# Output projection in fifteen products per unit for seven per pair of hidden tiles, with sums that read one operand from PSUM and a new written order

## The chip, the cores and the metric

One core of a Trainium2 chip runs the whole program. The metric is device time in microseconds (us) of one execution, the median of three runs. Engines are called TensorE (PE in the profile, its weight loads PEld), VectorE (DVE), ScalarE (ACT), GpSimd (POOL) and SyncE (SP, which here only issues DMAs).

## The reference, cut to what matters

```python
# x: (8, 4096, 192), weight: (8, 7); 32768 tokens in all
w = softmax(weight, axis=-1)                 # 8 heads of 24 channels, 7 taps
y[b, s, h] = sum_k w[h, k] * x_pad[b, s + k, h]   # causal depthwise convolution
xn = y / sqrt(mean(y * y) + 1e-6) * rms_g    # over the 192 channels
g, val = xn @ w_gate, xn @ w_val             # 192 -> 1536 each
out = (g * sigmoid(g) * val) @ w_out         # 1536 -> 192
```

All in float32 on the chip; the weights of the second block come as float64 and are converted at the start.

## The kernel before, in words

The tokens are worked in 32 pairs of two token tiles of 512 (T). Pair 0 is done plainly (L1060, L1101) behind the setup; pairs 1 to 31 go through one loop that follows a written order, `ORDER`. A pair's hidden width of 1536 is 12 tiles of 128, taken as four units of three tiles.

**Input stage.** A unit's gate and val sums (3 blocks of 64 channels by 3 hidden tiles by 2 token tiles, 18 block products) are made by 15 products of sums, `Unit.product` (L798). Gate uses the lower 64 rows of the array and val the upper 64, so that the two run side by side. The moving operands are the blocks of xn in `xb` (six: three channel blocks by two token tiles) and ten sums of them in `xc`, written `X0` to `X10` in the order (`x_sum`, L705 to L709): on GpSimd (`G`), on VectorE (`V`), or by a copying DMA from SP and an accumulating DMA that GpSimd issues (`Q`). The products accumulate in PSUM banks; half 0 is gate, half 1 val. Actions of `Unit.do` move between banks and tiles: `S` a snapshot of a bank (L747 on ScalarE, L751 on VectorE), `F` a copy from one bank into a new one, `D`, `C`, `N` and `R` sums on VectorE that take a bank and a tile (L814, L824, L818, L830), `G` a SiLU on ScalarE (L843) and `M` the multiplication of SiLU and val into the hidden tile `ht` (L850).

**Output stage.** Here 2x2 blocks (token tile by neighbouring hidden tiles, hidden tiles by column halves) are multiplied by 7 products for 8 in place of the plain way. Their left sides are hidden tiles and sums of them, made by `Pair.sum` (L968 to L970; `S1` to `S4` in the order), their right sides blocks of `w_out` and sums of them, made once (`out_sums`, L864). 42 steps, each of six matmuls of 384, 256 or 128 columns on four quarters of 32 columns of the array (`Pair.tile`, L938), accumulate in three banks X, Y, Z. `c1`, `s7`, `c2` copy among them, `C22` and `C21` join (L991), `T11` to `T22` turn 32x32 blocks into row order (L953), and `st0`, `st1` store.

**Work ahead.** In the same order, VectorE makes the convolution of the pair after the next (`cv`, L476, seven taps by three parts that accumulate in three PSUM banks), then `sq` (ScalarE), `red`, `pow` (GpSimd), `bc`, `mul` (GpSimd, L530) make the norm, `place` stores it to DRAM, and `fetA`, `fetB` load the next pair's blocks into `xb` (L696).

**Order.** A word of `ORDER` is an engine letter, an action, a half and a unit (`GM1.0.2`: GpSimd, multiplication of hidden tile 1 of unit 2). `p2` issues the next two of the pair's products. A minus sign at the end means that the action belongs to the pair before. Each engine runs its own instructions in the order in which they are written, and waits only where data or buffers ask for it; so the order of words sets each engine's queue, not the time. `D` words go to SP's queue. PSUM has eight banks in two groups of four (`free`), handed out as the order is written.

Of the kernel before, what the change touches and what calls it, by code (L numbers as in the profile page):

```python
# [19 lines left out]
def kernel(  # L20
# [99 lines left out]

# [1197 lines left out]
```

## Time and profile before

| quantity | value |
|---|---|
| median of 3 runs | 2594.6 us (2593.61 to 2594.77) |
| span of the profiled execution | 2591.7 us |
| the same execution's idle TensorE | 11.4 us (busy 2580.3) |
| VectorE, ScalarE, GpSimd busy | 2273.3, 1554.2, 2078.6 us |
| granted clock of TensorE | 1.000 |
| first pair of the loop starts | 125.77 us |
| products of TensorE by line, share of the chain | L798 62%, L938 32%, L1060 2%, L1101 1% |

The span runs from the first to the last instruction; the median lies 2.9 us above it, and this is taken as fixed. The chain that ended last follows the work back from the last instruction, at each step to what released it. A group's mean time is that of one instruction from its start to its end; successive instructions of an engine overlap, so the time from start to start is shorter.

### The profile page before, as it was taken

The numbers are of one execution on the slowest core, as the hardware profiler recorded it, in microseconds if no ns is written. First come the engines' busy times: TensorE is split into PE (matmuls) and PEld (weight loads), VectorE is DVE, ScalarE is ACT, GpSimd is POOL, SyncE is SP. The second block draws the span as 40 slices with busy tenths as digits, with TensorE's granted clock in tenths as the row PEclk, the third lists the DMA queues.
The fourth block names the chain that finished last, engine by engine and source line by source line (L and its number), as shares of the span: only waits on it lengthen the run. The fifth ranks groups of instructions, "written<-read, shape, count | busy, mean of one in ns | idle before, by whom it ended". The sixth has DMA issues, their size and how long they took to land.

```text
span 2591.7 us, 61274 instructions
## 1 busy us (share of the span) xinstructions
PE 2580.3 (100%) x23872; PEld 1777.6 (69%) x23872; DVE 2273.3 (88%) x3681; ACT 1554.2 (60%) x2825; POOL 2078.6 (80%) x1791
## 2 busy tenths in 40 slices
PE   9999999999999999999999999999999999999999
PEld 6876666767667666676666676666766666766666
DVE  8899989888889988889889889898988898898975
ACT  6566555675555765556755557655567555676554
POOL 4887788887778877788877888778888788887777
PEclk9999999999999999999999999999999999999999
DMA  6243554334553335443345433354433455334431
GB/s 145 57 83 59 100 100 87 75 65 90 100 100 77 72 68 104 99 83 77 65 91 100 98 76 69 74 104 96 86 76 66 92 100 94 72 72 80 91 76 22
DMA packets 555887, 216.54 MB, mean 84 GB/s; under 512 B 488782, under 2 KB 491342, under 8 KB 555598
## 3 DMA queue, kind: packets, MB, share of 16 engines
q1 hardware_dynamic: 525644, 164.00, 30.7%
q0 software_dynamic: 26208, 47.72, 10.9%
q8 instruction: 187, 3.06, 0.5%
q10 hardware_dynamic: 3746, 0.92, 0.2%
q14 instruction: 102, 0.84, 0.1%
HBM read 83.84 MB, written 49.55 MB: 51 GB/s over the span
## 4 chain that ended last, share of the span: by engine, by line
PE 98%; DMA 1%; POOL 0%; DVE 0%; issue 0%; SPq 0%; DVEq 0%; POOLq 0%
PE ps L798 62%; PE ps L938 32%; PE ps L1060 2%; PE ps L1101 1%; DMA xb<-xd 0%; POOL tls L970 0%; DMA xc<-xb 0%; DVE xb L647 0%; POOL more L970 0%; SPq L696 0%; DVE wf L338 0%; POOL xc L706 0%; DVE xc L333 0%; DVE o_sb L953 0%; DVE xc L298 0%
## 5 line engine op out<-in xcount | busy, mean ns | idle before, releaser
L798 PE MATMUL ps<-xc,wf 64*128 64x512 f32 x4960 | 1214.6, 591 | 0.0
L798 PEld LDWEIGHTS ps<-xc,wf 64*128 64x128 f32 x4960 | 681.6, 186 | 375.3 <-issue 161.8
L798 PE MATMUL ps<-xb,wf 64*128 64x512 f32 x2480 | 680.3, 591 | 0.0
L747 ACT ACTIVATE tile<-ps 128x512 f32<-128x512 f32 x678 | 391.0, 593 | 388.3 <-PE ps L798 282.7
L747 ACT ACTIVATE tls<-ps 128x512 f32<-128x512 f32 (+1 forms) x562 | 323.5, 588 | 438.9 <-PE ps L798 209.9
L850 POOL TENSOR_TENSOR ht<-ht,tile 128x512 f32<-128x512 f32 x329 | 419.2, 1278 | 125.4 <-ACT tile L843 48.9
L798 PEld LDWEIGHTS ps<-xb,wf 64*128 64x128 f32 x2480 | 354.2, 187 | 182.7 <-issue 91.9
L970 POOL TENSOR_TENSOR early<-ht 128x512 f32<-128x512 f32 x279 | 374.7, 1343 | 42.2 <-DMA ht<-ht 37.3
L850 POOL TENSOR_TENSOR ht<-ht,tls 128x512 f32<-128x512 f32 x260 | 331.2, 1279 | 76.9 <-ACT tls L843 33.2
L747 ACT ACTIVATE ps<-ps 128x512 f32<-128x512 f32 (+1 forms) x589 | 336.1, 581 | 87.6 <-PE ps L938 32.5
L476 DVE SCALAR_TENSOR_TENSOR ps<-xh,tp,ps 128x512 f32<-128x512 f32 x450 | 320.6, 750 | 3.9 <-ACT ps L468 1.7
L938 PE MATMUL ps<-ht,wo_sb 128*32 128x128 f32 (+2 forms) x5208 | 318.3, 380 | 0.0
L938 PEld LDWEIGHTS ps<-ht,wo_sb 128*32 128x32 f32 x5208 | 233.8, 110 | 81.7 <-issue 22.0
L938 PE MATMUL ps<-ht,x 128*32 128x128 f32 (+2 forms) x4464 | 250.7, 379 | 0.0
L830 DVE TENSOR_TENSOR tile<-ps,tile 128x512 f32<-128x512 f32 x349 | 237.8, 684 | 10.2 <-PE ps L798 5.4
L830 DVE TENSOR_TENSOR ht<-ps,tile 128x512 f32<-128x512 f32 x328 | 223.0, 682 | 6.4 <-ACT tile L747 6.4
L938 PEld LDWEIGHTS ps<-ht,x 128*32 128x32 f32 x4464 | 184.4, 110 | 61.2
L843 ACT ACTIVATE tile<-tile 128x512 f32<-128x512 f32 x349 | 214.5, 625 | 0.0
L830 DVE TENSOR_TENSOR ht<-ps,tls 128x512 f32<-128x512 f32 x292 | 199.4, 683 | 6.8 <-ACT tls L747 3.6
L830 DVE TENSOR_TENSOR tls<-ps,tls 128x512 f32<-128x512 f32 x271 | 185.2, 685 | 16.7 <-PE ps L798 13.6
L938 PE MATMUL ps<-early,x 128*32 128x256 f32 (+2 forms) x3348 | 196.0, 379 | 0.0
L938 PEld LDWEIGHTS ps<-early,x 128*32 128x32 f32 x3348 | 143.0, 110 | 44.6
(152 smaller groups left out, 3270.2 us busy)
## 6 DMA issues: line engine op xcount, KB each, us to landing
xb<-xd SPq DMA_DIRECT2D x120, 384.0 KB
xc<-xb SPq DMA_DIRECT2D x120, 256.0 KB
xd<-yn SPq DMA_DIRECT2D x244, 96.0 KB
xh<-in_x_dram SPq DMA_DIRECT2D x192, 105.0 KB
ht<-ht POOLq DMA_DIRECT2D x62, 256.0 KB, 3.3
xc<-xb POOLq DMA_DIRECT2D x60, 256.0 KB, 3.8
xc<-xc POOLq DMA_DIRECT2D x60, 256.0 KB, 4.0
out_dram<-o_sb SPq DMA_DIRECT2D x122, 96.0 KB
```

What stands on the lines that cost most here:

```text
L476: nc.vector.scalar_tensor_tensor(out=dst, in0=xk, scalar=w, in1=at, op0=ALU.mult, op1=ALU.add)
L747: nc.scalar.activation(out=dst, in_=src, func=AF.Copy, scale=float(s))
L798: nc.tensor.matmul(out=self.new(v, h, True) if first else self.old(v, h), lhsT=wf[self.u][HALF[h], WAT[i], :], rhs=x_op(XOP[i])[HALF[h]], ...
L830: nc.vector.tensor_tensor(out=self.hv(v) if h else t[:], in0=self.old(v, h), in1=t[:], op=plus(s))
L843: nc.scalar.activation(out=t[:], in_=src[:], func=AF.Silu)
L850: engine[eng].tensor_tensor(out=self.hv(v), in0=src, in1=t[:], op=ALU.mult)
L938: nc.tensor.matmul(out=self.bank(b)[i * Q : (i + 1) * Q, at : at + n], lhsT=left, rhs=cols, start=fresh, stop=True, skip_group_check=True, ...
L970: engine[eng].tensor_tensor(out=dst, in0=a, in1=b, op=op)
L1060: nc.tensor.matmul(out=bank(h, bks[h])[:], lhsT=wf[u][HALF[h], AT[h][k] * NF + f, :], rhs=xb[HALF[h], g, k, :], start=(k == 0), stop=(k == ...
L1101: nc.tensor.matmul(out=bank(h, bks[h])[:, w : w + D], lhsT=hts[f // NF][HALF[h], g, f % NF, j * P : (j + 1) * P], rhs=wo_sb[HALF[h], f, :] ...
```

## The change

The output stage goes over to 15 products per unit in place of 18: two token tiles by three hidden tiles by three column blocks of 64. A unit's six hidden tiles are called a to f. A product is four matmuls of 256 columns, one for each quarter; there are 60 in a pair, in the order of `OUTS`. They accumulate in K, R, N and four half banks C0, C1, C3, C4; `FORKS` copy among these, `SNAP` takes snapshots and `JOIN` adds them in. The left sides are made by `SUMS`: by GpSimd (`G`), by an accumulating DMA (`Q`), or by VectorE (`P`), which then takes its second operand from a PSUM bank into which ScalarE has copied it (`Ak...`). The same goes for two of the sums of x (`AkX3 PX3`, `AkX6 PX6`). Two val results of the last unit stay in their bank (`W`) until they are multiplied. Eleven sums of blocks of `w_out` are made in 18 steps, 12 ahead of pair 1 and 6 in it.

```diff
+    PLACE = {'a': 1, 'b': 0, 'c': 2, 'd': 4, 'e': 3, 'f': 5}
+    BANKS = {'K': 1, 'R': 1, 'N': 0, 'C01': 1, 'C34': 0}
+    OUTS = (
+        "11.1 11.0 6.0 6.2 4.1 6.1 6.3 11.2 4.2 1.0 1.2 11.3 4.0 4.3 14.3 9.0 8.0 8.1 8.2 9.1 9.3",
+        "9.2 14.2 14.1 5.0 8.3 10.0 5.3 10.3 5.1 5.2 3.1 13.2 13.1 3.3 7.0 7.3 13.0 10.1 7.1 10.2",
+        "7.2 13.3 1.3 14.0 12.0 3.0 2.1 12.1 12.3 12.2 1.1 3.2 0.3 2.2 2.0 0.1 0.2 2.3 0.0",
+    )
     ORDER = (
...
+        "VD6- VD0- GX5- GX10- p1 VT2- p1 GX9- VD2- VD3- VT4- p2 VT5- Asq- AS40.0.0 p2 AS40.1.0",
+        "VT3- p1 AF0.0.0 VT0- GX8- p1 VT1- VC.0.0 GX7- AF0.1.0 p3 VC.1.0 AS41.0.0 AS41.1.0 p1",
+        "AS00.0.0 p2 AS00.1.0 p2 GX4- p1 Vred- VD5.1.0 AS42.0.0 VD5.0.0 p1 AS42.1.0 VR1.0.0",
+        "VR0.0.0 Gpow- VR1.1.0 AS51.0.0 p1 AS51.1.0 p1 VR0.1.0 p1 Dload- Vbc- AF2.0.0 p1 AG0.0.0",
...
+        "AG4.0.0 GM2.1.0 VR5.1.0 VM4.1.0 AG3.0.0 p1 AF0.0.1 p1 GM3.1.0 p2 Gcb.0 p1 VS41.0.1 p1",
...
+        "VR5.1.3 AG5.0.3 p2 Qde.2 VR3.0.3 Qbe.2 AG4.0.3 VM4.1.3 p1 WR3.1.3 AG2.0.3 AG3.0.3 p1",
+        "Akp4.2 p2 GM1.1.3 VM3.1.3 p2 GM0.1.3 Akab.3 Akp9.0 Pp4.2 p2 AS6 GM5.1.3 Pab.3 p1 WR2.1.3",
+        "Gdf.3 Dplace- Akp4.0 Gde.3 Acv0_1 p2 DfetA DfetB p1 Pp4.0 p1 AF3 Gp4.3 Akp9.1 VM2.1.3",
+        "Qp9.2 p1 Pp9.0 Vcv1_1 Pp9.1 Gcb.3 p1 Gp9.3 p1 Vcv2_1 AF1 p1 Vcv3_1 Vcv4_1 p2 Akabe.1",
+        "Akbe.1 Vcv5_1 p1 Pabe.1 p2 Gabe.0 Gabe.2 p2 AF0 Acv0_2 Vcv6_1 p1 Qbe.3 p1 Pbe.1 p1",
+        "Vcv1_2 Akbce.0 p1 Qabe.3 p1 VS8 p3 AkX3 p1 Pbce.0 p1 AS5 Vcv2_2 p1 Gbce.3 Akbcf.1 Vcv3_2",
+        "PX3 p1 Gbce.2 p2 Gbce.1 Vcv4_2 p1 Vcv5_2 Vcv6_2 Acv0_0 Gbcf.0 QX0 Vcv1_0 Akabd.1 p2",
+        "Pbcf.1 Qabd.0 p2 AS7 Pabd.1 p2 Vcv2_0 Gbcf.2 p1 AS13 p2 Akbcf.3 Pbcf.3 VD13 AkX6 Akabd.2",
+        "p2 Qabd.3 p1 Vcv3_0 Vcv4_0 Pabd.2 Vcv5_0 p2 AF4 p1 Vcv6_0 p2 VD1 p1 GX1 p3 VD7 AS2 PX6",
+        "GX2",
     )
...
@@ x_sum
+        if eng == "A":
+            staged[i] = stage(x_op(b))
+            return
         e = nc.gpsimd if eng == "G" else nc.vector
+        e.tensor_tensor(out=xc[:, d, :], in0=x_op(a), in1=unstage(staged, i, x_op(b)), op=ALU.add)
+    def stage(src):
+        h = 0 if len(free[0]) >= len(free[1]) else 1
+        at = h, pick(h, False)
+        nc.scalar.copy(out=bank(*at)[:], in_=src)
+        return at
...
@@ Unit.do
+                stay = eng == "W"
+                dst = self.old(v, h) if stay else self.hv(v) if h else t[:]
+                nc.vector.tensor_tensor(out=dst, in0=self.old(v, h), in1=t[:], op=plus(s))
+                if not stay:
+                    self.leave(v, h)
...
+    VSUM = (
+        ("p11", "add", "01", "20"), ("p5", "sub", "11", "p11"), ("p8", "sub", "10", "p11"),
...
+    LEFT = {
+        11: ("X", "K"), 9: ("X", "K"), 5: ("CB", "K"), 7: ("CB", "K"), 12: ("CB", "K"),
+        4: ("S", "R"), 8: ("AB", "R"), 13: ("AB", "R"), 2: ("AB", "R"),
+        6: ("e", "N"), 1: ("b", "N"), 3: ("a", "C0"), 10: ("c", "C1"), 14: ("d", "C3"),
+        0: ("f", "C4"),
+    }
+    SUMS = {
+        "ab": ("AB", "a", "b"), "cb": ("CB", "c", "b"), "be": ("b", "b", "e"),
+        "df": ("X", "d", "f"), "de": ("X", "X", "e"), "p4": ("S", "AB", "X"),
+        "p9": ("X", "X", "CB"), "abe": ("AB", "AB", "e"), "abd": ("AB", "AB", "d"),
+        "bce": ("CB", "CB", "e"), "bcf": ("CB", "CB", "f"),
+    }
+    FORKS = {"F3": ("C3", "K", -1), "F1": ("C1", "R", 1), "F0": ("C0", "K", 1), "F4": ("C4", "K", -1)}
+    SNAP = {"S6": "N", "S8": "R", "S5": "K", "S13": "R", "S7": "K", "S2": "R"}
+    JOIN = {
+        "D0": ("C0", "S8", 1), "D1": ("C1", "S5", 1), "D13": ("N", "S13", -1),
+        "D7": ("N", "S7", -1), "D3": ("C3", "S2", -1), "D2": ("K", "S2", 1), "D6": ("K", "S6", -1),
+    }
...
@@ Pair.products
+            for w in " ".join(OUTS).split():
+                n, u = (int(i) for i in w.split("."))
+                src, b = LEFT[n]
...
+                cols, to = self.form(src, u), self.part(b)
+                for q in range(NQ):
+                    i, a = divmod(q, 2)
+                    nc.tensor.matmul(
+                        out=to[q * Q : (q + 1) * Q, :], lhsT=left[:, u, a],
+                        rhs=cols[:, i * HALFT : (i + 1) * HALFT], start=fresh, stop=True,
+                        skip_group_check=True, tile_position=(0, q * Q),
+                    )
+                yield
...
@@ Pair.sum
+            if name[0] == "k":
+                self.staged[name[1:], u] = stage(self.form(SUMS[name[1:]][2], u))
+                return
+            dst, a, b = (self.form(i, u) for i in SUMS[name])
+            b = unstage(self.staged, (name, u), b)
             if eng == "Q":
+                nc.gpsimd.dma_start(out=dst, in_=b, accum_op=ALU.add)
                 return
+            engine[eng].tensor_tensor(out=dst, in0=a, in1=b, op=ALU.add)
```

The parts of a convolution take their PSUM banks from the groups 1, 0, 0 for 0, 1, 0; the order of pair p + 1's first words is the one shown first, right behind the last.

## The prediction

> **What bounds the kernel now.** I read the page first, then the chain that ended last, then the busy time of each engine in one pair (the one that starts at 760.77 us) and in its two stages, then VectorE's and GpSimd's order of time there. First the page's busy times:
>
> ```profile
> PE 2580.3 (100%) x23872; PEld 1777.6 (69%) x23872; DVE 2273.3 (88%) x3681; ACT 1554.2 (60%) x2825; POOL 2078.6 (80%) x1791
> ```
>
> TensorE is never idle, and the row of granted clock is 9 in all slices, so nothing is lost to the clock. The chain in order of time has two pieces per pair:
>
> ```profile
> 760.77 51.92 PE ps L798 x240
> ...
> 892.06 27.44 PE ps L938 x337
> ```
>
> The gate and val products (L798) take 51.92 us, the output products (L938) 27.44 us, together 79.36 us, in pair after pair: 31 x 79.36 = 2460 of 2591.7 us. The stages, by window (columns: length, then busy us of TensorE, weight loads, VectorE, ScalarE, GpSimd):
>
> ```profile
> 760.77:812.69 51.92, 51.92 (x244) 32.99 (x248) 45.61 (x75) 41.49 (x77) 41.10 (x33) 1.00 0.31 50
> 812.69:840.13 27.44, 27.44 (x507) 21.03 (x506) 26.88 (x39) 6.60 (x11) 23.32 (x23) 1.00 0.66 154
> ...
> 1554.39:1633.75 79.36, 79.36 (x747) 54.03 (x746) 68.74 (x113) 48.08 (x87) 64.17 (x54) 1.00 0.42 84
> ```
>
> VectorE and GpSimd have 11 and 15 us to spare in a whole pair, but VectorE is nearly full in the output stage. Part of that is no work. VectorE's order of time there:
>
> ```profile
> 828.13 0.68 DVE L709 TENSOR_TENSOR xc<-xb 128x512 f32<-128x512 f32 x1
> 828.85 3.38 DVE L709 TENSOR_TENSOR xc<-xb,xc 128x512 f32<-128x512 f32 x1
> ...
> 832.95 1.96 DVE L709 TENSOR_TENSOR xc<-xb,xc 128x512 f32<-128x512 f32 x1
> ```
>
> The same size of sum takes 0.68, 3.38 and 1.96 us: the long ones read two SBUF tiles while GpSimd works on its own. GpSimd's own pace:
>
> ```profile
> 821.84 1.27 POOL L850 TENSOR_TENSOR ht<-ht,tile 128x512 f32<-128x512 f32 x1
> 823.07 1.28 POOL L970 TENSOR_TENSOR nt<-ht 128x512 f32<-128x512 f32 x1
> 824.31 2.53 POOL L970 TENSOR_TENSOR ht<-ht,early 128x512 f32<-128x512 f32 x2
> ```
>
> Starts lie 1.235 us apart when nothing holds it (1.23, 1.24). By the same reading VectorE starts a 128x512 operation every 0.60 us, a tap (L476) every 0.66, ScalarE a copy out of PSUM every 0.49, one out of SBUF some 0.55.
>
> **The change part by part, by pair.**
>
> *TensorE.* Before, 42 steps in the output stage each stream 384 columns through four quarters in two passes: 27.44 / 84 = 0.3267 us a pass, of which 384 columns at the pace of L798 (51.92 / 120 = 0.4327 us for a pass of 512) explain all but some 6 ns: 0.8333 ns a column and 6.6 ns a pass fit both rows. After, 60 products of 256 columns, two passes each: 120 x (0.2133 + 0.0066) = 26.40 us. Gain 1.04 us. Weight loads fall from 504 to 480, 55 ns apart instead of 54, so no new limit there. The L798 part keeps its 240 instructions. A pair without holds then takes 51.92 + 26.40 = 78.32 us; 31 x 1.04 = 32.2 us.
>
> *VectorE.* I count the written order. 512-wide operations: 76 in the units and 14 sums with a staged operand, 90 x 0.60 = 54.0; 18 taps x 0.66 = 11.9; eight 256-wide joins and one-off copies at 0.33 (the 384-wide join of 0.55 less 128 columns at 1.05 ns, less the overlap) = 2.7; six transposes at 0.32 = 1.9; reduce and the small ones 2.4. Sum 72.9 us. Before, the same count gives 68.1 (rows: 68.74, and 72.49 in the pair with the long sums). The joins are two-sided: a 256-wide one shown nowhere cannot cost less than its columns, 0.27, nor more than a 512-wide one, 0.60, so -0.5 to +2.2 us for the eight; I take 0.33, being nearest to the 384-wide row. That a PSUM operand is not dearer is seen in the multiplications of L850: 690 ns out of PSUM, 682 out of SBUF.
>
> [...]
>
> *ScalarE.* 16 more full copies (14 stagings) and nine 256-wide ones at 0.3 for three 384-wide ones: 48.1 + 9.1 + 2.7 - 1.2 = 58.7 of 78.3 us. Ample.
>
> *GpSimd.* This is the critical count. 49 sums and multiplications of 128x512 (18 M, 23 forms, 8 sums of x; before 19 + 22 + 2 = 43) x 1.235 = 60.5; the scaling 2.85; the power and its copies 2.5; ten DMA issues. An issue costs 0.61 between two sums (791.82 to 792.43) and about 1.2 behind another issue: some 8.1. Sum 74.0 us of 78.3, against 64.2 of 79.36. GpSimd may idle 4.3 us a pair; before it idled 15.2. In the output stage alone: 17 sums and 6 issues, 21.0 + 4.5 = 25.5 of 26.4 us.
>
> *What waits for it.* Walking GpSimd's queue with these paces and the readiness of its inputs as in before (first multiplication 10.5 us into the pair; wait for unit 2's first SiLU to about 36.5 us; from there no gap), the last sums come within half a microsecond of the product that needs them: `Gp9.3` ends about 60.1 to 60.6 us (product 9.3 is due at 60.7), `Gbce.1` 68.2 to 68.9 (7.1 due at 68.6), and `GX10` of the next pair, with `GX1 GX2 GX5` ahead of it, at 78.2 to 79.2, where TensorE wants it 0.87 us into its pair, at 79.2. The accumulating DMAs (3.3 us to landing) have 0.5 to 1 us.
>
> *Turnarounds on TensorE's path.* `F3` copies K negated into C3 right after product 11.3, and 14.3, two products later, must wait for it: product end, about 0.25 us to ScalarE (in before 1.15 us pass from a product's start to the copy's), 0.3 copy: 0.1 to 0.3 us late. `F1` behind it holds 8.0 by about as much. At the pair's start `Asq-` (1.49 us) now stands ahead of `AS40.0.0`; the copies `F0` end at 3.1 to 3.9 us where TensorE enters that bank at 3.5: 0 to 0.3. Together 0.1 to 0.9 us; I take 0.4. VectorE has about 1 us over when it makes `PX6`, which the first product of the next pair reads. In sum I take 0.4 us of holds a pair and GpSimd as just in time: 78.72 us.
>
> *Fetches and stores.* `Dplace-` and both fetches stand late in the order, but SP runs ahead: in before the fetch is issued when xb's last reader is done (51.8 us into the pair), so nothing moves. Nothing is added.
>
> *Ends.* Pair 1 now makes 18 weight sums of 256 columns for 12 of 192 (0.60 each, so some 0.75): 6 us more, covered, as pair 1 has no sums of x, power and scaling (about 13 us) in GpSimd's queue; 0 to 2 us if the first multiplication (now at 135.92, 0.19 of wait) comes late. In the tail seven short VectorE operations and a snapshot follow the last product (some 3 us, before 0.75), and both halves of the output go out behind it instead of one (768 KB for 384, about 2.3 us more traffic): 3 to 6 us, I take 4.
>
> *Sum.* 2591.7 - 31 x 0.64 + 4 = 2575.9 us of span; the median of the runs is 2.9 us over the span (2594.6), so 2579. Bounds of the same case: holds of 0.1 to 0.9 us, 2567 to 2595.
>
> **The rivals.** (1) *GpSimd becomes the bound; slower.* If its unavoidable idle exceeds 4.3 us a pair, every microsecond over goes to TensorE. For it: in the old order it idled 15.2 us, in spots such as 3.1 us before the scaling and 1.0 to 1.8 us at SiLUs, and x's sums now close a ring from one pair to the next. Against it: x's sums and the DMA issues are just what fills those spots. At 6 to 8 us of idle a pair takes 80.0 to 82.0: 2594.6 + 31 x 0.64 (or 2.64) + 4 = 2618 to 2680; the point from which it costs the gain is 5.2 us of idle. (2) *No holds.* ScalarE and GpSimd always in time, as before where TensorE is never idle: 2594.6 - 32.2 + 4 = 2566. (3) *The hand-over between pairs.* VectorE, with 24.0 of 26.4 us in the output stage, makes PX6 and frees banks (`T2`, `T4`, `T5`) about 1 us late: 79.3 us a pair, 2597, no change. (4) *Output not shortened*, because the quarters cannot keep 55 ns a load: at the old 27.44 us, with the holds, 2611; weight loads cover only 21 of 27.44 us, so it is unlikely.
>
> **How the numbers follow.** Forecast 0.43 (most of it faster), no holds 0.13, GpSimd as the bound 0.34, hand-over 0.08, not shortened 0.02. The likeliest is 2579. A measurement of this kernel tells some 0.2%, 5 us, from no change. Below 2589.4: 0.13 and 0.39 of the forecast's case: 0.52. Within: 0.09. Above: 0.39. The range goes from 2564 to 2624, which leaves out the long end of GpSimd's case and little below; the likeliest case's own is 2567 to 2595.
>
> **What would show it.** Right: pieces of L938's successor of 26.4 to 27 us, L798's of 52 to 52.4; GpSimd's busy share from 80 to about 93%; VectorE's sums at 0.69 us without long ones; short waits of TensorE for ScalarE copies near 14.3 and 8.0. Wrong: TensorE idle of over 1 us a pair with GpSimd's sums (`early`, `xc`) as releaser means rival 1; idle at the first product with `xc` by VectorE means 3; output pieces of 27.4 us without idle mean 4.

## The result, and the profile after

The changed kernel takes 2605.05 us (median of six runs, 2600.15 to 2610.69) against 2594.44 for the kernel before, run beside it (2592.70 to 2595.05): ratio 1.0044, interval 1.0032 to 1.0055. It is slower by 0.44%; the forecast of 2579 us was wrong in sign. The profiled execution took 2604.8 us, its span 2602.9, at a granted clock of 0.999.

The page of the changed kernel, first the busy times, then the chain that ended last by line:

```profile
PE 2564.1 (99%) x23128; PEld 1467.9 (56%) x23128; DVE 2424.1 (93%) x4056; ACT 1877.9 (72%) x3505; POOL 2398.9 (92%) x2104
...
PE 71%; POOL 15%; DMA 5%; issue 3%; DVE 2%; ACT 2%; SPq 0%; POOLq 0%; DVEq 0%; ACTq 0%
```

TensorE has 16 us less work than before, and in the loop the chain now leaves it: 15% of the span runs over GpSimd, 5% over transfers. In the changed kernel L823 are the gate and val products, L1002 the output products, L877 the multiplications of SiLU and val, L1027 the sums of hidden tiles, L1025 the accumulating DMAs. One pair by stage, pair 8, with the columns of before (length, then busy us of TensorE, weight loads, VectorE, ScalarE, GpSimd):

```profile
688.88:741.15 52.27, 52.27 (x245) 28.00 (x241) 49.07 (x84) 44.62 (x82) 48.76 (x43) 1.00 0.38 66
741.15:767.64 26.49, 26.25 (x481) 15.18 (x480) 26.10 (x43) 14.02 (x30) 25.60 (x23) 1.00 0.66 132
```

Three engines fill the output stage to 96% and more (VectorE 26.10, GpSimd 25.60 of 26.49). Before, in the same pair, VectorE had 1.3 and GpSimd 3.8 us over. What TensorE waits for (line, releaser: us in the whole span, times, longest us):

```profile
PE ps L1002 <- POOL nt L1027: 9.8, 32, 1.3
PE ps L1002 <- DMA more<-early: 7.1, 6, 3.0
PE ps L1002 <- DMA early<-ht: 5.3, 8, 0.9
```

The kernel before has no such row for its output products. The first row is mostly product 9.3, which comes 0.43 us late in all pairs but one (0.23 in pair 11); the second is 9.2, which reads the buffer that an accumulating DMA fills; the third is mostly 2.0. That one is not spread evenly: 2.0 is held by 0.7 to 1.0 us in every third pair (3, 6, 9 and so on to 30; not in 12, 0.24 in 27) and not at all in the others. In those pairs the DMA that makes its left side lands after 5.2 to 6.0 us, elsewhere after 3.6 to 4.9.

**Account, execution against execution.** Pair lengths are read from the first product of a pair to the first of the next; a product of the output stage is held by as much as its start lies more than 0.437 us behind the start of the one before it. Before, the 28 pairs other than 1, 12, and 31 (the last) take 79.39 us on average; now 79.30 (input 52.27, output 27.03). Pair 1 goes from 79.90 to 87.29, pair 12 from 79.36 to 83.72. So: pair 1 +7.4, pair 12 +4.4, the 28 others -2.5, the last pair -0.8, and from the last matmul's start to the end of the span 8.0 us for 5.3, +2.7. Sum +11.2, as the spans differ.

### The profile page after: what moved, and what is told of

It reads as the page before. It is cut to its first block, busy times and chain, and to the rows that moved or that the text cites. A ratio compares the mean times of both kernels' runs of the same rounds, so it can differ in the third digit from the quotient of the medians.

```text
span 2602.9 us, 61832 instructions
## 1 busy us (share of the span) xinstructions
PE 2564.1 (99%) x23128; PEld 1467.9 (56%) x23128; DVE 2424.1 (93%) x4056; ACT 1877.9 (72%) x3505; POOL 2398.9 (92%) x2104
## 4 chain that ended last, share of the span: by engine, by line
PE 71%; POOL 15%; DMA 5%; issue 3%; DVE 2%; ACT 2%; SPq 0%; POOLq 0%; DVEq 0%; ACTq 0%
PE ps L823 51%; PE ps L1002 16%; POOL ht L877 5%; POOL nt L1027 3%; POOL early L1027 3%; PE ps L1110 2%; DMA early<-ht 2%; DMA more<-early 2%; PE ps L1151 1%; POOL tls L1027 1%; DMA xb<-xd 1%; POOL more L1025 1%; POOL more L1027 1%; ACT ps L772 0%; ACT ps L726 0%
## 5 line engine op out<-in xcount | busy, mean ns | idle before, releaser
L823 PE MATMUL ps<-xc,wf 64*128 64x512 f32 x4960 | 1398.1, 592 | 0.9 <-ACT tile L772 0.8
L823 PEld LDWEIGHTS ps<-xc,wf 64*128 64x128 f32 x4960 | 683.2, 187 | 462.4 <-issue 269.6
L823 PE MATMUL ps<-xb,wf 64*128 64x512 f32 x2480 | 864.9, 590 | 0.0
L772 ACT ACTIVATE tile<-ps 128x512 f32<-128x512 f32 (+1 forms) x749 | 416.3, 572 | 201.9 <-PE ps L1002 100.1
L823 PEld LDWEIGHTS ps<-xb,wf 64*128 64x128 f32 x2480 | 375.9, 187 | 241.0 <-issue 179.5
L772 ACT ACTIVATE ps<-ps 128x512 f32<-128x512 f32 (+1 forms) x713 | 383.1, 546 | 176.8 <-PE ps L1002 148.2
L877 POOL TENSOR_TENSOR ht<-ht,tile 128x512 f32<-128x512 f32 x312 | 438.8, 1471 | 22.0 <-ACT tile L869 21.1
L1002 PE MATMUL ps<-ht,x 128*32 128x256 f32 x5952 | 413.0, 380 | 0.0
L877 POOL TENSOR_TENSOR ht<-ht,tls 128x512 f32<-128x512 f32 x246 | 349.0, 1468 | 22.8 <-ACT tls L869 22.0
L1027 POOL TENSOR_TENSOR early<-early,ht 128x512 f32<-128x512 f32 x248 | 351.3, 1527 | 0.0
L1027 POOL TENSOR_TENSOR early<-ht 128x512 f32<-128x512 f32 x248 | 342.7, 1382 | 4.8
L1002 PE MATMUL ps<-early,x 128*32 128x256 f32 x4216 | 278.9, 379 | 0.1
L1002 PEld LDWEIGHTS ps<-ht,x 128*32 128x32 f32 x5952 | 192.1, 110 | 130.1 <-DVE ht L877 4.9
L726 ACT COPY ps<-ht 128x512 f32<-128x512 f32 x248 | 145.3, 589 | 60.2 <-DVE y L482 44.9
L1002 PEld LDWEIGHTS ps<-early,x 128*32 128x32 f32 x4216 | 136.6, 110 | 91.9 <-ACT ps L772 5.0
L869 ACT ACTIVATE tls<-tls 128x512 f32<-128x512 f32 x276 | 171.8, 625 | 6.0 <-DVE tls L857 3.6
```

Source lines behind the costliest of these rows:

```text
L726: nc.scalar.copy(out=bank(*at)[:], in_=src)
L772: nc.scalar.activation(out=dst, in_=src, func=AF.Copy, scale=float(s))
L823: nc.tensor.matmul(out=self.new(v, h, True) if first else self.old(v, h), lhsT=wf[self.u][HALF[h], WAT[i], :], rhs=x_op(XOP[i])[HALF[h]], ...
L869: nc.scalar.activation(out=t[:], in_=src[:], func=AF.Silu)
L877: engine[eng].tensor_tensor(out=self.hv(v), in0=src, in1=t[:], op=ALU.mult)
L1002: nc.tensor.matmul(out=to[q * Q : (q + 1) * Q, :], lhsT=left[:, u, a], rhs=cols[:, i * HALFT : (i + 1) * HALFT], start=fresh, stop=True, s ...
```

## The experiments

The kernels are variants of the changed one. The table gives the median, the ratio to the kernel before with its interval, and, from each profiled execution, the mean of the same 28 pairs (input + output stage) and pairs 1 and 12. Each run was timed beside runs of the kernel before on the same chip (medians 2593.9 to 2594.5); the groups are later9 to unload, nostage to moved6, moved2 to moved3, moved2v to moved2s, afters to moved2sq, and moved2x.

| run | median us | ratio | 28 pairs | pair 1 | pair 12 |
|---|---|---|---|---|---|
| changed kernel | 2605.05 | 1.0044 (1.0032 to 1.0055) | 52.27 + 27.03 | 87.29 | 83.72 |
| later9 | 2596.36 | 1.0009 (1.0001 to 1.0018) | 52.42 + 26.75 | 83.74 | 82.07 |
| fetb | 2635.05 | 1.0158 (1.0144 to 1.0172) | 52.76 + 27.74 | 83.66 | 82.28 |
| wsum | 2610.91 | 1.0062 (1.0049 to 1.0074) | 52.29 + 26.94 | 93.20 | 82.38 |
| unload | 2592.21 | 0.9993 (0.9984 to 1.0002) | 52.50 + 26.62 | 86.21 | 80.19 |
| nostage | 2880.97 | 1.1103 (1.1085 to 1.1122) | 52.35 + 36.38 | 91.35 | 88.92 |
| unstay | 2650.23 | 1.0221 (1.0200 to 1.0242) | 52.28 + 28.82 | 84.38 | 85.04 |
| moved | 2621.05 | 1.0105 (1.0090 to 1.0120) | 52.22 + 27.77 | 83.79 | 81.78 |
| moved6 | 2623.65 | 1.0108 (1.0093 to 1.0124) | 52.23 + 27.74 | 83.47 | 81.41 |
| moved2 | 2603.92 | 1.0033 (1.0019 to 1.0047) | 52.51 + 26.71 | 83.60 | 82.69 |
| moved2f | 2605.61 | 1.0037 (1.0024 to 1.0050) | 52.74 + 26.89 | 81.69 | 81.28 |
| moved3 | 2602.84 | 1.0040 (1.0026 to 1.0054) | 52.45 + 26.92 | 82.96 | 81.88 |
| moved2v | 2595.67 | 1.0004 (0.9995 to 1.0013) | 52.66 + 26.62 | 83.80 | 81.95 |
| afterv | 2601.61 | 1.0025 (1.0016 to 1.0035) | 52.24 + 27.12 | 86.10 | 81.90 |
| moved2s | 2593.01 | 0.9991 (0.9982 to 1.0000) | 52.50 + 26.52 | 83.21 | 82.47 |
| afters | 2601.39 | 1.0027 (1.0015 to 1.0039) | 52.29 + 27.00 | 85.82 | 82.23 |
| moved2su | 2584.83 | 0.9962 (0.9949 to 0.9976) | 52.53 + 26.42 | 83.03 | 79.38 |
| moved2sq | 2623.95 | 1.0111 (1.0097 to 1.0125) | 52.77 + 27.44 | 83.44 | 80.21 |
| moved2x | 2598.09 | 1.0013 (1.0004 to 1.0022) | 52.44 + 26.85 | 85.67 | 81.32 |

Where a median and its profile's pairs disagree by a few us, the lead-in (the work ahead of pair 1) is the likely reason: in three of the profiles (unstay, moved6, moved2) pair 1 starts 6 to 7 us late. Just these three have a long copy of three columns on GpSimd at the start, here in the profiles of moved2 and moved2s by order of time; no edit touches it, and why it is long is open:

```profile
8.46 7.79 POOL L226 COPY ht<-x 128x3 f32<-128x3 f32 x1 [6.92 <-DMA x<-in_x_dram]
```

```profile
8.65 0.32 POOL L226 COPY ht<-x 128x3 f32<-128x3 f32 x1 [7.10 <-DMA x<-in_x_dram]
```

### The order of products

By the chain of what released what, the hold at 9.3 is the end of a path from the last input product. In pair 10 it reads, in order of time (start, length, what):

```profile
899.69 1.64 ACT tile L869 x3
901.32 1.01 ACT ps L726 x2
902.33 0.67 DVE tls L1027
...
905.41 0.69 DVE early L1027
906.10 0.04 issue
906.13 1.59 POOL early L1027
907.73 0.07 issue
907.80 1.29 POOL nt L1027
909.08 0.04 issue
909.13 17.59 PE ps L1002 x320
```

SiLUs and two staging copies on ScalarE, VectorE's sums, then two GpSimd sums (`Gcb.3`, `Gp9.3`); the last ends 0.05 us before 9.3 starts. GpSimd's own queue comes to the same point at the same time. The same stretch in its order of time:

```profile
899.88 1.60 POOL L877 TENSOR_TENSOR ht<-ht,tile 128x512 f32<-128x512 f32 x1
901.56 1.29 POOL L1027 TENSOR_TENSOR nt<-ht 128x512 f32<-128x512 f32 x1
902.93 1.29 POOL L1027 TENSOR_TENSOR nt<-nt,ht 128x512 f32<-128x512 f32 x1
904.30 1.30 POOL L1027 TENSOR_TENSOR tls<-early,nt 128x512 f32<-128x512 f32 x1
905.53 0.87 POOL L1025 DMA_DIRECT2D more<-early  x1
906.13 1.58 POOL L1027 TENSOR_TENSOR early<-ht 128x512 f32<-128x512 f32 x1
907.80 1.28 POOL L1027 TENSOR_TENSOR nt<-nt,early 128x512 f32<-128x512 f32 x1
```

Two of these sums read the result of the one just before and start 1.37 us behind it, where sums that do not depend on each other start 1.235 apart; from the sum behind the DMA issue to `Gp9.3`, which reads it, it is 1.67, and the multiplication at the top takes 1.68 up to the next start, as GpSimd comes late to it.

```diff
 # later9
-  ... 8.2 9.1 9.3  9.2 14.2 14.1 5.0 8.3 10.0 5.3 ...
+  ... 8.2 9.1 14.2 14.1 9.3 9.2 8.3 10.0 5.0 5.3 ...
```

> The changed kernel with products 9.3 and 9.2 moved two products later (behind 14.2 and 14.1) and 5.0 moved behind 8.3 and 10.0; nothing else. Theory A (a product stands too close behind the sum it needs: 9.3 waits 0.43 us in every pair for Gp9.3, which follows Gcb.3 and VectorE's VM2.1.3; 9.2 waits 0 to 0.7 us for an accumulating DMA): both holds go and the pair falls from 79.2 to 78.6 to 78.8 us, 12 to 18 us in all, 2587 to 2593. Theory B (GpSimd's queue is full and sets the period): the hold only moves to a later product (7.1, 2.0 or the next pair's first), and the time stays at 2600 to 2607.

Measured 2596.36 us, between the two. The hold at 9.3 is gone, and most of that at 9.2; pair 1 is 3.6 us shorter, pair 12 1.7. But all 28 other pairs now wait 0.29 us at 10.0 (C0 and C1 share a bank, and `F0` has to copy K after 9.2), and more often at the pair's first products: they gain 0.14 us a pair.

```diff
 # moved: ... 8.1 14.2 9.1 14.1 9.3 9.2 8.2 8.3 10.0 5.0 ..., and 2.0 behind 0.1 0.2
 # moved2: 8.2 in its place, 14.0 as cover
+  ... 8.2 9.1 14.2 14.1 9.3 9.2 8.3 14.0 10.0 5.0 5.3 ... 1.3 12.0 ... 2.2 0.1 0.2 2.0 2.3 0.0
 # moved3: moved2, and
-  2.2 0.1 0.2 2.0 2.3 0.0
+  2.2 0.1 2.0 2.3 0.2 0.0
```

> Order of the output products alone: 14.2 and 14.1 ahead of 9.3 and 9.2, then 8.2 and 8.3 between 9.2 and 10.0, 5.0 (the earlier run with 9.3 and 9.2 moved left a new hold of 0.29 us at 10.0, since only one product lay between 9.2 and 10.0), and 2.0 behind 0.1 and 0.2. Theory A (holds by place of products whose sums are late): no hold at 9.3, 10.0 or 2.0, 0.6 to 0.9 us a pair less than the changed kernel, and 9.2 in pairs 1 and 12 still held by about 2 us: 2583 to 2593 us. Theory B (something else paces the pair, holds only change their place): 2594 to 2601 us, as the earlier run with 9.3 and 9.2 moved, or above.

> The run moved, mended: there 8.2 stood behind the sum that overwrites its operand, so it waited for that sum and read it (its 1.2 us a pair were of the edit's own making). Here 8.2 keeps its place; 14.2 and 14.1 go ahead of 9.3 and 9.2, 8.3 and 14.0 lie between 9.2 and 10.0, and 2.0 goes behind 0.1 and 0.2. Theory A (each hold is a product whose sum is late; given other products to run, TensorE loses nothing): no hold at 9.3, 10.0 or 2.0, 9.2 held by 1.5 us in pairs 1 and 12 alone; the output stage 26.0 to 26.4 us, 2579 to 2588 us. Theory B (the pair is paced elsewhere and holds move on): 2592 to 2600 us.

> As moved2, with 2.3 one product earlier (0.1 2.0 2.3 0.2 0.0), so that ScalarE can empty the R bank earlier; the next pair's first val product writes that bank and starts 0.14 us behind the gate product in the changed kernel, and the two halves end the input stage 0.43 us apart, which costs 0.27 us at the change to the output stage. Theory S (the bank's release makes the skew): the first val product starts with the gate's, the input stage falls from 52.19 to 52.0 to 52.1 us, 3 to 6 us less than moved2. Rival (the skew has other makers, or 2.3 waits for its own sum): moved2 within 2 us, or more.

`moved` and moved6 (below) put 8.2 behind the sum that overwrites its operand, so that one product of unit 2 reads another sum; 2621.05 us holds 1.2 us a pair of waiting for it. moved2 does what was meant: no hold at 9.3, 10.0 or 2.0. By its pairs, 79.22 us, it gave nothing over later9 (79.17): theory B, though with its late lead-in the median lies above that theory's range. The time came back as 0.3 us at the first products of a pair (input stage 52.51 us; a pair without such holds has 52.19), 0.22 at 2.3 and 0.24 at 2.2, 12.2 and 12.3 together. In moved3 the first val product does start with the gate product (0.007 us apart, in the other versions 0.142), as theory S had it; but the halves still end the input stage 0.43 us apart, later banks make that up again, 2.3 and 2.0 wait more, and the pair takes 79.37 us. Half of theory S fell.

### The accumulating DMA behind the fetch

Pairs 10 and 12 of the changed kernel, GpSimd's issue for 9.2 (L1025) and SP's second fetch (L702), from the order of time of each engine:

```profile
905.53 0.87 POOL L1025 DMA_DIRECT2D more<-early  x1
...
1065.07 0.87 POOL L1025 DMA_DIRECT2D more<-early  x1
```

```profile
906.15 1.52 SPq L702 DMA_DIRECT2D xb<-xd  x2
...
1064.66 1.23 SPq L702 DMA_DIRECT2D xb<-xd  x2
```

In pair 10 the issue comes 0.62 us ahead of the fetch, in pair 12 0.41 us behind. The chain then reads:

```profile
1065.07 7.15 DMA more<-early
1072.22 0.04 issue
1072.26 9.90 PE ps L1002 x177
```

7.15 us to landing; the page's median for these DMAs is 3.9. Only pairs 1 and 12 lose this order, and only they hold 9.2 by over 3 us (3.18 and 3.15). Behind the fetch it lands after 7.17 us in pair 1 and 7.15 in pair 12, in the others after 3.3 to 4.7; what in the transfers makes the difference is not shown.

```diff
 # fetb: the second fetch behind the landing of Qp9.2 (moved2f: on moved2, behind the sum Gcb.3 next to it)
-  ... DfetA DfetB ... Qp9.2 ...
+  ... DfetA ... Qp9.2 DfetB ...
-  nc.sync.dma_start(out=mark[:, 0:1], in_=xb[HP : HP + 1, 1, 0, 0:1])
+  nc.sync.dma_start(out=mark[:, 0:1], in_=regs[REG["X"] * NU + 2][HP : HP + 1, 0:1])
```

> The changed kernel with the second fetch of xb (DfetB) made to wait for the landing of Qp9.2's accumulating DMA in place of the first fetch's landing, about 3 us later. Theory A (in two of 31 pairs the fetch is issued just ahead of Qp9.2 and its packets go first, and 9.2 is held 3.2 us): no pair has 9.2 held over 1 us, the two long pairs (1 and 12 of the profile) lose 3 us each, the total falls by 4 to 10 us to about 2598, and the runs lie within 3 us of one another in place of 10. Theory B (Qp9.2 is late only because GpSimd issues it late): pairs with a late issue keep their 3 us, no change. If the later fetch holds QX0 and with it the first products of the next pair, the time rises by up to 1 us a pair.

> As moved2, and the second fetch waits for GpSimd's sum that stands right behind the accumulating DMA for 9.2, so that the DMA is issued ahead of the fetch in every pair, at 1.5 to 2 us of delay of the fetch. Theory A (the order of the two issues decides whether 9.2 is held; the fetch has room): no hold at 9.2 in pair 1 or 12, 3 us less than moved2. Rival (the fetch has no room; what comes behind it is late, as in the earlier run in which it waited for the landing): up to 1 us a pair more, moved2 + 10 to + 30 us.

Both took every hold at 9.2 away: how the two issues lie to each other decides. It is a matter of degree: in unstay (below), where this DMA is issued later, it landed after 3.6 to 4.0 us where it came 0.66 us or more ahead of the fetch, after 4.4 to 4.8 at 0.12 to 0.39 us ahead, and after 5.3 to 7.4 where it came less than that ahead or behind. Both runs lost more than they gained, fetb 1.2 us a pair (12.2 held 0.64 us, the input stage 0.49 longer), moved2f 0.4 us a pair over moved2: the fetch has no room, since the DMA for X0 that reads what it brings stands in GpSimd's queue ahead of `Gbcf.2`, and the other sums of x behind it.

### Pair 1

```diff
 # wsum: all 18 weight sums, on moved6 (order of moved) only the last 6
-  nc.gpsimd.tensor_tensor(out=dst, in0=right(a), in1=right(b), ...)
+  nc.vector.tensor_tensor(out=dst, in0=right(a), in1=right(b), ...)
```

> The changed kernel with the 18 weight sums made by VectorE in place of GpSimd, at the same places. Theory A (pair 1 is 8 us longer because GpSimd, with 18 weight sums ahead of and in it, is late): pair 1 falls from 87.3 to 79.5 to 82 us, the total by 5 to 8 us to about 2598. Theory B (pair 1 is long only by the order of a fetch and an accumulating DMA): 0 to 3 us less.

> As the run moved, and the last 6 of the 18 weight sums, those that fall into pair 1, on VectorE in place of GpSimd. Theory A (GpSimd's six sums in pair 1 make its later work 7 us late, and VectorE has room for 6 x 0.7 us there): pair 1 3 to 5 us shorter than in moved, 2579 to 2590 us. Rival (VectorE, 93% busy, passes the 4 us on to the input products, as it did with all 18): pair 1 as long as in moved or up to 3 us longer.

wsum: the output stage of pair 1 falls from 33.38 to 26.37 us, so GpSimd's 18 sums are what made it long, the hold at 9.2 among it; its input stage grows from 53.92 to 66.83. moved6: output 30.34 to 27.18, input 53.46 to 56.29. Neither GpSimd nor VectorE has room for these sums at that place.

### The two other parts of the change

```diff
 # nostage: ORDER without its Ak... words    # unstay
-  Akp4.2, Akab.3, Akp9.0, ...               -  WR3.1.3, WR2.1.3
                                             +  VR3.1.3, VR2.1.3
```

> Leaves the nine or so ScalarE copies into PSUM out, so that VectorE's sums take both operands from SBUF (the order, the 15 products and all else as in the changed kernel). Theory A (the copies pay: they take the contention with GpSimd's sums away): VectorE's P sums go from 0.68 us to between 0.8 and 3.4 us each, as the two-SBUF sums of before did beside GpSimd's; with some 10 of them a pair VectorE loses 3 to 10 us, its sums land late and products wait for them: 2620 to 2760 us. Rival (the copies buy nothing, or cost ScalarE time and an extra hand-over that is itself what holds the products): 2590 to 2605 us, as late as or earlier than the changed kernel.

> The late val tiles leave their bank as SBUF copies again (VectorE copies WR2, WR3 as VR), so the last two multiplications of a pair take both operands from SBUF; all else as in the changed kernel. Theory A (staying in the bank takes the copy out of the chain from the end of the input stage to product 9.3): one copy of 0.4 to 0.6 us is back in that chain, the hold at 9.3 grows from 0.43 to about 0.8 to 1.0 us in every pair: 2612 to 2625 us. Rival (the chain has slack, the part is worth nothing): 2600 to 2610 us.

Both cost more than any theory gave; the copies that nostage leaves out are 14 a pair. VectorE's sums by form (line, names, count: shortest/median/longest ns), in the changed kernel and in nostage:

```profile
L1027 DVE TENSOR_TENSOR early<-early,ps x217: 673/680/690, 184.5 to 2589.8; 128x512 f32<-128x512 f32 x109
```

```profile
L1027 DVE TENSOR_TENSOR early<-early,ht x186: 676/1198/4924, 192.1 to 2865.5; 128x512 f32<-128x512 f32 x186
```

With both operands in SBUF the shortest still takes 676 ns, the median 1198, the longest 4924; with one in PSUM all lie between 673 and 690. nostage waits for them:

```profile
PE ps L1002 <- DVE early L1027: 152.2, 75, 6.2
PE ps L1002 <- DVE nt L1027: 49.2, 29, 1.7
```

So the copies into PSUM take the long sums away; in this order they are worth some 276 us. The prediction read from the 3.38 us row that the long sums run beside GpSimd's own, and the trace of before bears that out: of the 150 sums of x that VectorE makes in the loop out of two SBUF tiles (L709), the 115 with no 128x512 operation of GpSimd beside them take 647 to 696 ns, and the 25 that take 1310 to 3851 all run beside one for over 1 us. Not all of the 276 us is waiting (the mean granted clock of nostage is 0.980, for 0.999 in the changed kernel): behind the long hold at 2.1 in pair 9, TensorE's granted clock reads 0.50 for 3 us (913 to 916 us), and four products there take 0.85 us each for 0.43; over the pairs this makes about 1 us of the 9.4 that a pair loses. unstay shows the same in small, in the multiplications (L877) and in what TensorE waits for:

```profile
L877 DVE TENSOR_TENSOR ht<-ps,tile x68: 679/682/693, 230.7 to 2624.3; 128x512 f32<-128x512 f32 x68
...
L877 DVE TENSOR_TENSOR ht<-ht,tls x30: 734/1252/2554, 186.7 to 2625.7; 128x512 f32<-128x512 f32 x30
```

```profile
PE ps L1002 <- DMA more<-early: 32.5, 24, 3.2
PE ps L1002 <- DVE ht L877: 19.5, 29, 1.4
```

The second row is 6.3, held by 0.78 us a pair; 9.3, where theory A looked for the loss, is held less than before (0.17). Some 0.5 us later in VectorE, the DMA for 9.2 is issued about 6.1 us into the output stage for 5.55, and so meets the fetch in most pairs instead of two.

### What paces a pair

```diff
 # unload: sums ab and cb of units 0 to 2 left out from pair 2 on (moved2su: the same on moved2s)
+  if name in ("ab", "cb") and u < 3 and self.p > 1:
+      return
 # moved2v, afterv: moved2 and the changed order without three taps
-  Vcv3_2 Vcv4_2 Vcv5_2
 # moved2s, afters: moved2 and the changed order with S8 on ScalarE
-  VS8
+  AS8
 # moved2sq: moved2s, and          # moved2x: moved2s, and input products 2 and 3 exchanged
-  Gabe.0 Gabe.2                   +  CHAINS[0][1:3] = CHAINS[0][2:0:-1]
+  Gabe.2 Qabe.0
```

> The changed kernel without the sums ab and cb of units 0 to 2 from pair 2 on (six GpSimd sums of 1.235 us a pair, 7.4 us, left out; the output then holds old sums). Theory B (GpSimd's load sets the period): all holds go and a pair takes about 78.2 us, 30 us less in all, 2575. Theory A (9.3 waits for a chain that starts at the end of the input stage): the 0.43 us at 9.3 stay, those at 9.2 and 2.0 mostly go, the pair takes 78.5 to 78.9, 2585 to 2595.

> As moved2, with three of VectorE's convolution taps (taps 3 to 5 of the third block) left out of the output stage: 3 x 0.66 = 2.0 us of VectorE a pair. Theory V (VectorE, busy without a gap from the change to the output stage up to the next pair's turns, sets when the next pair's first products get their banks): no hold at 2.2, 12.3 or at the next pair's first product, the output stage 25.9 to 26.1 us and the input stage 52.2, 0.6 to 0.8 us a pair less than moved2: 2578 to 2587 us. Theory G (GpSimd or the accumulating DMAs set it): moved2 within 5 us, 2598 to 2606.

> The changed kernel in its own order, with the same three taps left out. Theory V: the holds that VectorE makes go (the first product of a pair, 12.2, 2.2), those at 9.3 (0.43, earlier in the stage than the taps), 2.0 and at 9.2 in pairs 1 and 12 stay: 78.5 to 78.9 us a pair, 2590 to 2600 us; holds and VectorE's load have to be taken away together. If 2.0's hold goes too, VectorE makes that one as well. Theory G: 2600 to 2608.

> As moved2, and the snapshot S8 copied by ScalarE (14 of 26.4 us busy in the output stage) in place of VectorE: 0.33 us less for VectorE there, with nothing left out. Theory V: the next pair's first product comes 0.2 to 0.35 us earlier in pairs where nothing else holds it, 4 to 10 us less than moved2: 2594 to 2600 us. Rival: no less than moved2 within 3 us, or S8 comes later and 13.2 or D0 waits.

> The changed kernel in its own order, with only the snapshot S8 moved from VectorE to ScalarE. If VectorE's 0.33 us in the output stage alone were the loss: 10 us less than the changed kernel, 2593 to 2597 us. If the order's holds (9.3, 9.2, 2.0) and VectorE's end must be mended together: within 4 us of the changed kernel, 2600 to 2606 us, with the hold at 9.3 as before.

> As moved2s, with the sums ab and cb of units 0 to 2 left out from pair 2 on (6 sums, 7.4 us of GpSimd a pair), as in the run unload on the changed order. Theory G (after order and VectorE are mended, GpSimd's queue is what is late: the x sums that the next pair's second product reads, and the accumulating DMAs behind them): the hold of 0.3 us at the first products of a pair goes, 2.3 and 12.2 in every third pair shrink, pair 78.3 to 78.6 us where moved2s has 79.1: 2568 to 2582 us. Rival (the sums left out lie early in the pair, GpSimd's queue at the end of the output stage is set by what releases it there): moved2s within 5 us.

> As moved2s, with the sum abe of unit 0 made by an accumulating DMA in place of GpSimd's tensor_tensor (one issue of some 0.6 us for a sum of 1.24; product 13.0 reads it 5 us later): GpSimd 0.4 to 0.6 us less in the output stage, nothing left out. Theory G: the x sum is earlier by as much, the first products' hold of 0.3 us goes, 5 to 9 us less than moved2s: 2584 to 2588 us. Rival: the fourth accumulating DMA delays the others (1.3, 2.0, 2.3 wait longer): moved2s or up to 15 us more.

> As moved2s, with the second and third input product of each pair exchanged: the second read a sum of x that GpSimd makes last (it waits 0.3 us for it in most pairs of moved2s), the third reads x itself. Nothing is left out. Theory G (GpSimd's queue, not TensorE, sets the start of a pair): the hold of 0.3 us goes, as the sum has 0.86 us more, 6 to 9 us less than moved2s: 2584 to 2588 us. Rival (GpSimd's queue is full all through the output stage, the 0.3 us comes back at 2.3, 12.2 or 1.3, behind its later accumulating DMAs): moved2s within 3 us.

*VectorE.* afterv and afters gained little in the old order (2601.61 and 2601.39 us for 2605.05, in other groups of runs) and by the 28 pairs nothing (79.36 and 79.29 for 79.30): the hold at 9.3 lies ahead of that relief. On moved2 the relief shows, since with the early holds gone VectorE's queue is what remains: 2593.01 us for 2603.92, though part of this difference is moved2's late lead-in; by pairs it is 79.22 to 79.02, 5.6 us in 28. Where no product is late, the output stage of moved2s takes 26.04 us, against 26.37 in moved2. Theory V held for the stage, not for the first product. moved2v fits this: its VectorE has 2 us over, and the pair is no shorter (79.28 us; the median, 2595.67, lies between the ranges of both theories). The output stage of pair 8 in moved2s and in moved2v:

```profile
734.51:760.56 26.05, 26.05 (x482) 15.19 (x481) 25.66 (x42) 14.24 (x31) 25.66 (x24) 1.00 0.68 135
```

```profile
737.29:763.32 26.03, 26.03 (x481) 15.28 (x480) 24.02 (x40) 13.92 (x30) 25.64 (x24) 1.00 0.67 135
```

VectorE falls from 25.66 to 24.02; GpSimd stays at 25.64 of 26.03 and the next pair's second product waits for its sum of x as before.

*GpSimd.* In the changed order, 7.4 us less GpSimd work a pair brought 0.2 us a pair (unload). The hold at 9.3 falls from 0.43 to 0.14: GpSimd then stands 0.48 us ahead of the multiplication at the head of the rows above, which starts 52.13 us into pair 10 in both runs but takes 1.29 us for 1.60. So GpSimd's load made 0.3 us of that hold, and the path from the last input product with its sums that wait for each other the rest. But 2.0 falls only from 0.25 to 0.17, and 0.23 us come back at the pair's first products. The median fell by 12.8 us; in the profiles pair 12 gives 3.5 us and pair 1 1.1. On moved2s the same cut gains 8 us, but not in the ordinary pairs: of the sum over the pairs, 6.2 us, pair 12 gives 3.1 and pair 28 gives 1.9, the other 27 of the 28 nothing, pair 1 and the last pair the rest. The sums left out lie in the input stage; GpSimd's queue in the output stage begins when the last val results are there, and from there it has no gap in two pairs of three. Making that queue lighter with what is at hand failed twice. moved2sq turned a sum into a DMA and lost 31 us (12.2 waits in 26 pairs, 2.3 in 21). moved2x gave the last sum of x more time, and the hold at the first products shrank (0.11 us a pair for 0.30), but with the products exchanged the shortest input stage is 52.34 us for 52.19, and 2.3 and 9.2 are held longer. What TensorE waits for in moved2s (its weight loads, PEld, show the wait for the sum of x), then in moved2x (which is a line longer, so L1003 for L1002):

```profile
PE ps L1002 <- DMA early<-ht: 5.2, 10, 0.7
PE ps L1002 <- DMA more<-early: 3.9, 3, 1.6
...
PE ps L823 <- POOL xc L718: 1.2, 3, 0.5
```

```profile
PEld ps L823 <- POOL xc L718: 23.2, 38, 1.3
```

```profile
PE ps L1003 <- DMA early<-ht: 8.1, 16, 0.8
PE ps L1003 <- DMA more<-early: 6.8, 8, 2.0
```

```profile
PEld ps L824 <- POOL xc L718: 4.3, 9, 0.6
```

So the remaining loss, 1.2 us a pair in moved2s over 51.92 + 25.9, has several makers. At the first products (0.3 us) it is GpSimd's queue. In the output stage it is the landing of DMAs more than that queue: the pairs 3, 6, 9 to 30 (without 12) take 27.17 us there, the others but 1 and 28 take 26.11, with GpSimd's queue without a gap. In each of those nine GpSimd stands 0.3 to 1.1 us before it issues the DMA for X0, and the next accumulating DMA lands after 5.3 to 5.6 us in place of 4.4 to 4.8; 2.3 and 12.2 are held there and nowhere else in the 28. moved2su keeps this (27.11 and 26.10). What comes round every third pair was not found. The change from the input to the output stage (0.27 us, below) is the other part. A cut of GpSimd's sums inside the output stage alone wasn't run; that the floor would then be TensorE's 52 + 26 us is argued, not shown. The best of these versions with nothing left out, moved2s, is no more than level with the kernel before.

## Why the prediction was wrong, by its steps

**TensorE's own time: right in kind, better in size.** Forecast 26.40 us for 60 products; without any hold, in moved2s, the stage takes 26.04, of which 0.11 is the change to the next pair: 25.9. A product takes 0.432 us where the sum had 0.44; the 6.6 ns a pass taken from the old mix of widths did not carry over.

**Holds of 0.4 us a pair: the step that failed.** Measured 52.27 + 27.03 against 51.92 + 25.9, 1.5 us a pair. Of the 27 us by which the span missed the forecast 2575.9, the 28 pairs make 16 (79.30 us for 78.72; the shorter products hide part of the holds), and pairs 1 and 12, 8.6 and 5.0 us over 78.72, make 13.6. The tail and the last pair, shorter than forecast, take 1.7 off, and 1.2 more goes off because the pairs of before, from which the sum starts, were that much longer than 31 x 79.36. The places were wrong too: none is at 14.3 or 8.0, behind ScalarE's turnarounds. They are at 9.3 (0.43), 9.2 (0.13 without pairs 1 and 12), 2.0 (0.25), 4.3 (0.07), and the change from input to output stage (0.27). The prediction had 9.3 in its list: `Gp9.3` within half a microsecond of its product. Two things failed there. The walk of GpSimd's queue went at 1.235 us a sum also where a sum reads the one before (1.37, and 1.67 behind a DMA issue) and where GpSimd comes late to the last multiplications, so `Gp9.3` ends 61.4 us into the pair on average, not at 60.1 to 60.6. And "just in time" was taken as zero; but where several sums are just in time, the late ones count in full and the early ones give nothing back.

**The change of stage** was not in the sum. In the kernel before the gate and val halves start 0.007 us apart and end 0.15 apart; now the val half starts 0.14 us late, behind a bank that ScalarE empties (`S2`), ends up to 0.43 late, and the first output product needs both: 52.19 us in a pair without other holds, for 51.92. moved3 mended the start and not the end, so what makes the rest is open.

**Pair 1 "covered": wrong.** GpSimd is busy there for 52.84 of the 53.92 us of the input stage; the six further sums stand ahead of the pair's own, and the pair is 7.4 us longer than before. Its products 11.3 and 9.2 are held by 1.5 and 3.2 us, the DMA for 9.2 being issued 7.6 us into the stage, behind the fetch. Behind that hold the granted clock reads 0.50 for 3.4 us (193.6 to 197.0 us), and four products take 0.79 to 0.85 us each, 1.6 us more in all; behind the hold of the same length in pair 12 it reads 1.00.

**"Accumulating DMAs have 0.5 to 1 us", "nothing moves. Nothing is added": half right.** The fetch is where it was, but a new DMA is issued close to it (0.62 us ahead in pair 10), and in pairs 1 and 12, where the fetch comes first, 9.2 is held by over 3 us. The sum had 3.3 us to landing; the DMAs into `early`, of which 2.0 reads one, have a median of 4.6, and with 5.2 to 6.0 in every third pair the slack was gone.

**GpSimd 74.0 us a pair: right** (48.76 + 25.60 = 74.4 in pair 8), and the output stage of 25.5 us too. **VectorE 72.9: short** by 2.3 (49.07 + 26.10), with 26.1 in the output stage for the 24.0 of rival 3. **VectorE's sums**: 0.68 us without long ones, as forecast; the PSUM operand adds nothing that shows (680 ns, for 647 to 696 out of two SBUF tiles with no 128x512 operation of GpSimd beside them, in before). **Tail** 2.7 us for 4; in before the last store moves at 172 GB/s from 2588 to 2590 us, at which 384 KB take the 2.3 us that the prediction added.

**The rivals.** The length that rival 3 gave, 79.3 us a pair and 2597, is what later9 and the 28 pairs came to, but its mark (the first product waiting for `xc` by VectorE) is not among TensorE's waits in the trace of the change, and in its weight loads only seven times, 2.9 us in all; VectorE's end shows only once the earlier holds are taken away, and is worth 0.2 us a pair. Rival 1's idle limit was not passed (4.4 us in pair 8, limit 5.2). Its mechanism is there in places only: GpSimd's queue makes 0.3 us at 9.3 in this order and 0.3 us at a pair's first products in moved2s, not 1 to 3 us a pair.

**Left open:** pairs 12 and 28 are long in nearly all variants (in moved2s 82.47 and 80.12 us for 79.02), and the DMAs of every third pair land late. In pair 12 of the changed kernel GpSimd stands for 1.51 us at a DMA issue that names nothing it waits for; 16 pairs lie between it and pair 28. Why was not found for either.

## What to carry to other kernels

A shorter matmul stage gained nothing here, where two other engines already filled the stage: add up each engine's queue for the stage alone, from the event that opens it to its last consumer, take the pace of sums that depend on each other for those that do, and price "just in time" at what it is late, not at zero. Look at the holds pair by pair, since a mean hides a hold that falls in every third. Moving a late product behind others is worth trying, since it is cheap, but each hold taken away shows the next engine's; here order and a lighter VectorE had to be changed together, and even so only 12 us came back, the loss and no more. Before a one-off block of work is called covered, see whether its engine has a gap between that place and the first consumer.

## What the runs showed of the hardware

An accumulating DMA of 256 KB that GpSimd issues lands after a median of 3.3 to 4.6 us by its place in the kernel, and after 7.15 us when a fetch of two 384 KB parts was issued 0.41 us ahead of it. GpSimd's 128x512 sums start 1.235 us apart, and 1.37 where one reads the result of the one before. VectorE's 128x512 sum out of two SBUF tiles has a median of 1198 ns in nostage (186 sums, while GpSimd works on its own) and goes up to 4924; with no 128x512 operation of GpSimd beside it (before, 115 sums of x) it takes 647 to 696, and with one operand in PSUM (changed kernel) 217 such sums stay within 17 ns. Behind an idle of 3 us TensorE's granted clock read 0.50 for 3.4 us in pair 1 of the changed kernel and 1.00 in pair 12. A GpSimd copy of three columns at the very start took 7.6 to 7.8 us in three of the profiles and 0.2 to 0.4 in the others.
